# Window attention backward: the turn of P and dS of four quads moved from VectorE to a DMA transpose

## The chip, the cores and the metric

One core of a Trainium2 chip runs the program. The metric is the device time of one execution in microseconds (us); the figure for a kernel is the median of its runs. The core's engines are TensorE (PE in the profile; its weight loads are PEld), VectorE (DVE), ScalarE (ACT), GpSimd (POOL) and SyncE (SP). SP, ACT and POOL also issue DMAs. Each engine takes its instructions strictly in the order of its own queue.

## The reference

The input x is a 256 x 256 image with 384 channels in bf16, cut into 1024 windows of 8 x 8 = 64 tokens. Each window has its own one-head attention:

```
q, k, v = xw @ wqkv            # (64, 384) each
p = softmax(q @ k.T * 384**-0.5)
out = (p @ v) @ wo
```

The kernel computes `out` (out_0) and, from `grad_out`, the gradients of x (out_1), wqkv (out_2) and wo (out_3).

## The kernel before

The 1024 windows are taken in 128 *quads*. A quad is four tiles of 128 tokens, and a tile is two windows, one in partitions 0 to 63 (LO) and one in 64 to 127 (HI). The weights are multiplied together once at the start, so that the loop works with x, the output gradient d, and four 384 x 384 products A, AT, B, BT.

The order on every engine is written by hand (`manual_schedule`, L436), so each engine's queue is the program order of its instructions. The loop (L456) is a software pipeline. Step i works on three quads: A = quad i+1 is projected (y and z, L155), B = quad i gets its scores, its softmax and its u and v (L180, L192, L227), C = quad i-1 gets its attention (L254). A fourth, quad i+3, is loaded. Within a step (L346) the order is:

- scores of B on TensorE; then the softmax steps `soft` 0 to 5 on VectorE, with the exponential on ScalarE, between the four tiles of u and v, whose PSUM results ScalarE evicts (L235)
- the projection of A with kind 0 (z, evicted by ScalarE, L165), the last softmax step and `turn(B)`
- the loads of quad i+3: half of x on SP's queue (L128), the gradient on POOL's queue (L129)
- a gather of z on VectorE (L173), the projection of kind 1 (y, evicted by ScalarE, L167), the other half of the x loads on ScalarE's queue (L133)
- if there is any, one block `gf_rows` of the weight gradient on TensorE (L308), added up by VectorE (L306)
- the attention of C in four slots (L254); between the slots come half-size blocks of the weight gradient (L316), again only if there are any, and the second gather on VectorE

At the start of step i, SP's queue gets the transposing DMAs of quad i+2 (`load_turn`, L135: dT from dq and xT from xq) and of quad i (`to_tokens`, L175: tok from zy). For the first four quads dT, and for quad 0 xT, are made on TensorE instead (L143).

The softmax of a quad leaves P (called Pb) and dS, the gradient of the scores, side by side in the tile `ps` (128 x 2 x 4 x 64, bf16). Attention also needs both transposed within each window. `turn` (L237) does that on VectorE with five STREAM_TRANSPOSE instructions, which turn blocks of 32 x 32: one over the whole tile (L240) puts the diagonal blocks right, and four (L244) the off-diagonal ones. The result is the tile `PS`. One slot of attention (L263) reads it through `operand` (L247) as PT and ST, each time 64 x 64 of one half of the partitions.

All PSUM results go through one ring of eight banks (L58). In a slot of attention ScalarE evicts pw to Wq (L280), po to o (L273) and most of the d tiles; VectorE evicts pu to Uq (L283) and the d tile of the first and third slot (L273). A product can start only when an eviction has freed a bank for it.

The weight gradient is taken in groups of GQ = 3 quads. In steps 0 to 3 no group is complete, so no `gf_rows` and no half blocks are there yet. In step 127 there is no quad to project any more.

Of the kernel before, what the change touches and what calls it, by code (L numbers as in the profile page):

```python
# [9 lines left out]
ALU = mybir.AluOpType  # L10
AX = mybir.AxisListType
BF16 = mybir.dt.bfloat16
F32 = mybir.dt.float32

P = 128
WIN = 8
WT = WIN * WIN
QUAD = 4
# [5 lines left out]
def kernel(  # L24
# [21 lines left out]
    nc = tc.nc  # L46
# [8 lines left out]
    qp = ctx.enter_context(tc.tile_pool(name="qp", bufs=2))  # L55
# [64 lines left out]
    LO, HI = slice(0, WT), slice(WT, P)  # L120
# [68 lines left out]
    def over_k(ap, n=P):  # L189
        return ap.unsqueeze(2).broadcast_to([n, QUAD, WT])  # L190

    def soft(st, step):  # L192
        sd = st["sd"]
        if step == 0:
            st["mx"] = mx = sm.tile([P, QUAD], F32, tag="mx", name="mx")
            for w, h in ((0, HI), (1, LO)):
                nc.vector.tensor_reduce(out=mx[h, :], in_=sd[h, :, w, :], axis=AX.X, op=ALU.max)
        elif step == 1:
            mx = st["mx"]
            st["sh"] = sh = sm.tile([P, QUAD, WT], F32, tag="sh", name="sh")  # L200
            for w, h, o in ((0, HI, LO), (1, LO, HI)):
                nc.vector.tensor_tensor(out=sh[o, :, :], in0=sd[h, :, w, :], in1=over_k(mx[h, :], WT),
                                        op=ALU.subtract)
        elif step == 2:
            st["ex"] = ex = sm.tile([P, QUAD, WT], F32, tag="ex", name="ex")
            nc.scalar.activation(out=ex[:], in_=st["sh"][:], func=ACT.Exp)
        elif step == 3:
            ex = st["ex"]
            rs = sm.tile([P, QUAD], F32, tag="rs")
            nc.vector.tensor_reduce(out=rs[:], in_=ex[:], axis=AX.X, op=ALU.add)  # L210
            ri = sm.tile([P, QUAD], F32, tag="ri")
            nc.vector.reciprocal(out=ri[:], in_=rs[:])
            st["ps"] = ps = qp.tile([P, 2, QUAD, WT], BF16, tag="ps", name="ps")
            st["Pb"], st["dS"] = ps[:, 0, :, :], ps[:, 1, :, :]
            nc.vector.tensor_tensor(out=st["Pb"], in0=ex[:], in1=over_k(ri[:]), op=ALU.mult)
        elif step == 4:
            st["pr"] = pr = sm.tile([P, QUAD, WT], F32, tag="pr", name="pr")
            for w, h in ((0, LO), (1, HI)):
                nc.vector.tensor_tensor(out=pr[h, :, :], in0=sd[h, :, w, :], in1=st["Pb"][h, :, :], op=ALU.mult)  # L219
            st["D"] = D = sm.tile([P, QUAD], F32, tag="D", name="D")  # L220
            nc.vector.tensor_reduce(out=D[:], in_=pr[:], axis=AX.X, op=ALU.add)
        else:
            pd = sm.tile([P, QUAD, WT], F32, tag="pd")
            nc.vector.tensor_tensor(out=pd[:], in0=st["Pb"], in1=over_k(st["D"][:]), op=ALU.mult)
            nc.vector.tensor_tensor(out=st["dS"], in0=st["pr"][:], in1=pd[:], op=ALU.subtract)

    def uv(st, t, part):  # L227
# [9 lines left out]
    def turn(st):  # L237
        ps = st["ps"]
        st["PS"] = dst = qp.tile([P, 2, QUAD, WT], BF16, tag="PS", name="PS")
        nc.vector.transpose(out=dst[:].rearrange("p s t k -> p (s t k)"), in_=ps[:].rearrange("p s t k -> p (s t k)"))  # L240
        for first in range(0, P, WT):
            for q in (0, SQ):
                k = SQ - q
                nc.vector.transpose(out=dst[first + k:first + k + SQ, :, :, q:q + SQ].rearrange("p s t k -> p (s t) k"),  # L244
                                    in_=ps[first + q:first + q + SQ, :, :, k:k + SQ].rearrange("p s t k -> p (s t) k"))

    def operand(st, n, t, h):  # L247
        if n in ("PT", "ST"):
            return st["PS"][h, int(n == "ST"), t, :]
        if n in ("z", "y"):  # L250
            return st["tok"][h, int(n == "y"), :, t, :]
        return st[n][h, t, :]

    def attend(st, t):  # L254
# [8 lines left out]
        def slot(bank, straight, crossed, start=False, stop=False):  # L263
            for h in (LO, HI):
                o = OTHER[h.start]
                products = [(h, bank, straight, {"start": True, "stop": True}),
                            (o, pd[h is LO], crossed, {"start": start, "stop": stop})]
                for o, dst, (lhs, rhs), flags in products if h == LO else products[::-1]:
                    nc.tensor.matmul(dst[o, :], lhsT=operand(st, lhs, t, h), rhs=operand(st, rhs, t, h), **flags)  # L269
# [76 lines left out]
    def step(c, b, a, ahead):  # L346
# [4 lines left out]
        C_, B, A = on(c), on(b), on(a)  # L351
        B(scores)
        B(soft, 0)
        if b is not None and c is None:
            weight_rest()
        B(uv, 0, 0)
        B(uv, 0, 1)
        B(soft, 1)
        B(uv, 1, 0)
        B(uv, 1, 1)  # L360
        B(soft, 2)
        B(soft, 3)
        B(uv, 2, 0)
# [4 lines left out]
        for mo in range(CK):  # L368
            A(project, 0, mo)
        B(soft, 5)  # L370
        B(turn)
        if ahead is not None:
            load(ahead, ON_ACT)
# [16 lines left out]
    ON_ACT = 2  # L390
    EV = {"z": "AAA", "y": "AAA", "u": "AAAA", "v": "AAAA", "o": "AAAA", "U": "DDDD", "W": "AAAA", "d": "DADAA"}
    quads = [(row, col) for col in range(0, W, WIN) for row in range(0, H, 2 * WIN * QUAD)]
    sts = [{"at": q, "i": i} for i, q in enumerate(quads)]
    n = len(sts)
    AHEAD = 3
    dw_out = out_2.rearrange("(m p) j -> p m j", p=P)
    dwo_out = out_3.rearrange("(m p) n -> p m n", p=P)
# [109 lines left out]
```

## Time and profile before

| | us |
|---|---|
| median of 3 runs | 1917.22 |
| lowest and highest run | 1910.97, 1922.25 |
| the profiled execution, its own time | 1913.78 |
| its span, from the first to the last instruction | 1912.0 |
| PE, DVE, ACT, POOL busy in the span | 1897.3, 1676.1, 1530.4, 860.0 |

The span is what the profile's lines refer to; 1.8 us lie around it. Times such as "at 42.11" count from the start of the span. A line of a group of instructions names the source line, the engine, the operation, the tiles (out<-in), their shapes and types and the count; behind the bars stand the busy time in us with the mean of one instruction in ns, and the idle time of that engine before these instructions with what ended it. A line of the timeline has the start, the duration, the engine and the instruction, and in brackets how long the engine waited before it and for whom. The granted clock is TensorE's, as a share of full speed. `ACTq` and `SPq` are the queues of DMA issues. "DMA to landing" is the time from the issue of a DMA to its last byte.

### The profile page before, as it was taken

What the parts mean: (1) busy time and instruction counts of PE and PEld (TensorE: products, weight loads), DVE (VectorE), ACT (ScalarE), POOL (GpSimd) and SP (SyncE); (2) the same over time, 40 slices, a digit from 0 to 9 for tenths busy, and PEclk for the clock granted to TensorE, in tenths of its full rate; (3) what the DMA queues carried; (4) which work ended last, traced back from release to release, by engine and by line L of the source; (5) the groups of instructions that cost most, each with busy time, mean ns of one, the idle gap of its engine ahead of it and who ended that gap; (6) DMA issues with size and microseconds to landing.
All of it is one profiled execution on the core that took longest, in us unless ns stands there. A gap on an engine that the chain in (4) does not pass through costs nothing.

```text
span 1912.0 us, 57287 instructions
## 1 busy us (share of the span) xinstructions
PE 1897.3 (99%) x22359; PEld 1131.5 (59%) x22359; DVE 1676.1 (88%) x3625; ACT 1530.4 (80%) x3357; POOL 860.0 (45%) x1574
## 2 busy tenths in 40 slices
PE   8999999999999999999999999999999999999998
PEld 5556655655665565556556655655665565556555
DVE  6888888888888888888888888888888888888887
ACT  7878887888788888878887887888788788878884
POOL 3444544444444444444444444444444444445432
PEclk9999999999999999999999999999999999999999
DMA  8999999999999999999999999999999999999993
GB/s 183 200 223 215 221 211 214 232 210 222 200 232 211 225 204 229 217 223 216 224 210 212 225 226 219 206 220 221 223 214 216 223 224 204 210 231 222 206 197 93
DMA packets 943376, 406.91 MB, mean 213 GB/s; under 512 B 825344, under 2 KB 918528, under 8 KB 943104
## 3 DMA queue, kind: packets, MB, share of 16 engines
q1 hardware_dynamic: 830352, 226.46, 77.1%
q0 software_dynamic: 75264, 151.11, 32.6%
q10 hardware_dynamic: 37488, 25.67, 6.0%
q8 instruction: 175, 2.87, 0.7%
q14 instruction: 97, 0.79, 0.1%
HBM read 101.84 MB, written 101.84 MB: 107 GB/s over the span
## 4 chain that ended last, share of the span: by engine, by line
PE 95%; DVE 2%; DMA 1%; ACT 1%; issue 0%; ACTq 0%; SPq 0%
PE pj L151 50%; PE pg L151 13%; PE ph L324 13%; PE sd L151 5%; PE pw L269 5%; PE po L269 4%; PE pu L269 4%; DMA dT<-dq 1%; PE pd L269 1%; DMA xq<-in_x_dram 0%; DVE PS L244 0%; ACTq L133 0%; PE pe L403 0%; DVE pr L219 0%; DVE Uq L283 0%
## 5 line engine op out<-in xcount | busy, mean ns | idle before, releaser
L289 POOL DMA_DIRECT2D out_dram<-o x512 | 274.4, 536 | 795.4 <-ACT o L273 783.6
L280 ACT CAST Wq<-pw 128x384 bf16<-128x384 f32 x512 | 246.6, 482 | 280.7 <-PE pw L269 264.9
L151 PEld LDWEIGHTS <-xT 128*128 128x128 bf16 x3072 | 292.3, 98 | 182.9 <-issue 1.0
L129 POOL DMA_DIRECT2D dq<-in_grad_out_dram x512 | 270.6, 534 | 194.5 <-PE pj L151 86.8
L151 PE MATMUL pj<-B_sb,xT 128*128 128x384 bf16 x1536 | 334.0, 327 | 0.0
L151 PE MATMUL pj<-AT_sb,xT 128*128 128x384 bf16 x1536 | 333.8, 326 | 0.0
L283 DVE CAST Uq<-pu 128x384 bf16<-128x384 f32 x512 | 283.1, 553 | 16.9 <-PE pu L269 4.9
L291 POOL DMA_DIRECT2D out_dram<-d x480 | 277.8, 579 | 16.3 <-ACT uq L235 6.6
L151 PE MATMUL pj<-dT,BT_sb 128*128 128x512 bf16 x1152 | 269.5, 379 | 0.0
L151 PE MATMUL pj<-xT,A_sb 128*128 128x512 bf16 x1152 | 269.5, 379 | 0.0
L269 PE MATMUL pd<-tok,ps 64*64 64x384 bf16 x2048 | 256.4, 327 | 0.7 <-ACT Wq L280 0.6
L165 ACT CAST yz<-pj 128x512 bf16<-128x512 f32 x384 | 224.8, 586 | 37.2 <-PE pj L151 28.6
L273 ACT CAST o<-po 128x384 bf16<-128x384 f32 x512 | 249.3, 487 | 3.8 <-PE po L269 3.6
L235 ACT CAST vq<-pj 128x384 bf16<-128x384 f32 x512 | 247.1, 483 | 3.7 <-PE pj L151 0.5
L235 ACT CAST uq<-pj 128x384 bf16<-128x384 f32 x512 | 244.4, 477 | 3.6 <-PE pj L151 1.8
L167 ACT CAST yz<-pj 128x512 bf16<-128x512 f32 x384 | 225.1, 586 | 23.5
L244 DVE STREAM_TRANSPOSE PS<-ps 32x256 bf16<-32x256 bf16 x512 | 223.2, 436 | 9.7
L151 PEld LDWEIGHTS <-xq 128*128 128x128 bf16 x1572 | 153.6, 98 | 115.0 <-issue 0.6
L324 PEld LDWEIGHTS <-xq 64*64 64x64 bf16 x6000 | 177.5, 107 | 67.0
L324 PE MATMUL ph<-Wq,xq 64*64 64x384 bf16 x3984 | 204.4, 322 | 0.0
L151 PEld LDWEIGHTS <-A_sb 128*128 128x128 bf16 x1152 | 112.7, 98 | 135.9
L151 PEld LDWEIGHTS <-BT_sb 128*128 128x128 bf16 x1152 | 112.7, 98 | 122.3
(85 smaller groups left out, 3066.1 us busy)
## 6 DMA issues: line engine op xcount, KB each, us to landing
dq<-in_grad_out_dram POOLq DMA_DIRECT2D x512, 96.0 KB, 5.8
out_dram<-o POOLq DMA_DIRECT2D x512, 96.0 KB, 5.1
out_dram<-d POOLq DMA_DIRECT2D x480, 96.0 KB, 5.4
xq<-in_x_dram SPq DMA_DIRECT2D x262, 96.0 KB, 4.9
xq<-in_x_dram ACTq DMA_DIRECT2D x250, 96.0 KB, 6.0
out_dram<-d POOLq DMA_DIRECT2D x64, 48.0 KB, 5.4
tok<-zy SPq DMA_TRANSPOSE x128, 10.3
xT<-xq SPq DMA_TRANSPOSE x127, 7.6
```

The costliest lines, as they stand in the source:

```text
L129: nc.gpsimd.dma_start(out=dq[:, t, :], in_=windows(grad_out, st, 2 * t))
L151: nc.tensor.matmul(out, lhsT=lhsT, rhs=rhs, start=start, stop=stop)
L165: ENG[EV["z"][mo]](out=yz[:, mo, :, 0:4:3, :], in_=pj[:])
L167: ENG[EV["y"][mo]](out=yz[:, mo, :, 1:3, :], in_=pj[:])
L235: cp(out=dst[:, t, :], in_=pj[:])
L269: nc.tensor.matmul(dst[o, :], lhsT=operand(st, lhs, t, h), rhs=operand(st, rhs, t, h), **flags)
L273: copies[EV[name][i]](out=sb[rows, :], in_=src[rows, :])
L280: copies[EV["W"][t]](out=st["Wq"][:, t, :], in_=pw[:])
L283: copies[EV["U"][t]](out=st["Uq"][:, t, :], in_=pu[:])
L289: nc.gpsimd.dma_start(out=windows(out_0, st, 2 * t), in_=o)
L291: nc.gpsimd.dma_start(out=windows(out_1, st, 2 * t - 1), in_=d if t else above[:])
L324: nc.tensor.matmul(dst[o, :], lhsT=st["xq"][h, t, ma * P + o.start:ma * P + o.stop], rhs=st["UW"[f] + "q"][h, t, :], start=(i == 0), stop= ...
```

## The change

For quads 0, 1, 2 and 127 (`crossed`) the five VectorE transposes go, and one transposing DMA on SP's queue takes their place. This DMA turns 128 x 128 blocks, that is, a whole tile with both windows at once. So its source is a new tile `cr` (one buffer), in which each of the four tiles has two blocks side by side, w = 0 and w = 1: P stands in its own half of the partitions, copied there by ScalarE, and dS in the *other* half, written there by VectorE with a second subtraction of the same operands. Turned, the partitions of each half hold P of one window and dS of the same window. `operand` picks them accordingly: in the upper half PT and ST have changed places. The plain dS in `ps` is still made, since attention uses it too.

```diff
@@ soft(), last step @@
             pd = sm.tile([P, QUAD, WT], F32, tag="pd")
             nc.vector.tensor_tensor(out=pd[:], in0=st["Pb"], in1=over_k(st["D"][:]), op=ALU.mult)
+            if st["crossed"]:
+                st["cr"] = cr = qp.tile([P, QUAD, 2, WT], BF16, tag="cr", name="cr", bufs=1)
+                for w, h, o in ((0, LO, HI), (1, HI, LO)):
+                    nc.scalar.copy(out=cr[h, :, w, :], in_=st["Pb"][h, :, :])
+                    nc.vector.tensor_tensor(out=cr[o, :, w, :], in0=st["pr"][h, :, :], in1=pd[h, :, :], op=ALU.subtract)
             nc.vector.tensor_tensor(out=st["dS"], in0=st["pr"][:], in1=pd[:], op=ALU.subtract)
@@ turn() @@
         st["PS"] = dst = qp.tile([P, 2, QUAD, WT], BF16, tag="PS", name="PS")
+        if st["crossed"]:
+            whole = dst[:].rearrange("p s t k -> p (s t k)").rearrange("p (t s k) -> p t s k", t=QUAD, s=2)
+            st["PS"] = whole.rearrange("p t s k -> p s t k")
+            nc.sync.dma_start_transpose(out=whole.rearrange("p t s k -> p t (s k)"),
+                                        in_=st["cr"][:].rearrange("p t w k -> p (t w k)"))
+            return
         nc.vector.transpose(out=dst[:].rearrange("p s t k -> p (s t k)"), in_=ps[:].rearrange("p s t k -> p (s t k)"))
@@ operand() @@
-            return st["PS"][h, int(n == "ST"), t, :]
+            return st["PS"][h, int((n == "ST") == (h == LO or not st["crossed"])), t, :]
@@ the list of quads @@
-    sts = [{"at": q, "i": i} for i, q in enumerate(quads)]
-    n = len(sts)
+    n = len(quads)
+    sts = [{"at": q, "i": i, "crossed": i < GQ or i == n - 1} for i, q in enumerate(quads)]
```

## The prediction

> **What bounds the kernel now.** I read the page's first part and its 40 slices, then TensorE's waits, then 5 us windows at both ends, then the chain and the engines' timelines there.
>
> ```profile
> PE 1897.3 (99%) x22359; PEld 1131.5 (59%) x22359; DVE 1676.1 (88%) x3625; ACT 1530.4 (80%) x3357; POOL 860.0 (45%) x1574
> ```
>
> TensorE (PE) is idle for only 1912.0 - 1897.3 = 14.7 us. All of this change must come from those, from stretches at a lower clock, or from new waits. The changed quads are 0, 1, 2 and 127, so the ends matter. In the windows the columns are the window, its length, busy PE, PEld, DVE, ACT, POOL, the granted clock, DMA share and GB/s:
>
> ```profile
> 40.00:45.00 5.00, 2.96 (x39) 1.54 (x35) 4.86 (x10) 3.47 (x9) 2.60 (x5) 0.77 1.04 212
> 45.00:50.00 5.00, 5.00 (x62) 3.92 (x61) 3.22 (x9) 4.27 (x11) 4.08 (x8) 0.89 1.07 200
> ...
> 55.00:60.00 5.00, 3.29 (x53) 1.66 (x53) 4.85 (x11) 4.17 (x11) 2.33 (x4) 0.97 1.19 127
> 60.00:65.00 5.00, 5.00 (x42) 3.20 (x40) 2.07 (x5) 3.34 (x9) 4.22 (x9) 0.69 1.13 217
> ...
> 70.00:75.00 5.00, 3.29 (x62) 1.80 (x62) 4.85 (x11) 4.12 (x11) 2.42 (x5) 1.00 1.18 231
> ```
> ```profile
> 1875.00:1880.00 5.00, 3.09 (x47) 1.55 (x49) 4.77 (x10) 1.35 (x3) 0.53 (x1) 0.90 0.16 49
> 1880.00:1885.00 5.00, 5.00 (x66) 3.34 (x59) 3.16 (x6) 3.42 (x8) 3.25 (x7) 0.76 0.34 93
> ```
>
> Four holes: 2.04 us in step 1, 1.71 in step 2, 1.71 in step 3, 1.91 in step 127, each with VectorE (DVE) full. After three of them the clock falls: weighting the windows, 5 x (0.23 + 0.11) = 1.7 us, 5 x (0.03 + 0.31) = 1.7 and 5 x (0.10 + 0.24) = 1.7 are lost, 5.1 in all. Idle and clock in the steps whose turn changes are 5.7 + 5.1 = 10.8 us, the most that can be won. The chain shows what ends the first hole (start, us, what):
>
> ```profile
> 38.35 0.72 DVE PS L240
> ...
> 40.44 0.44 DVE PS L244
> 40.91 0.56 DVE zy L173
> 41.50 0.56 DVE Uq L283
> 42.09 0.57 DVE d L273
> 42.70 0.48 PE pw L269
> ```
>
> The five turns of quad 1 stand in VectorE's queue ahead of the gather and of the first eviction of attention(0), and TensorE needs that PSUM bank. Its timeline says so in step 1 and in step 127:
>
> ```profile
> 42.11 0.32 PE L269 MATMUL po<-uq,PS 64*64 64x384 bf16 x1 [1.80 <-DVE Uq L283]
> ```
> ```profile
> 1878.97 0.46 PE L269 MATMUL pu<-xq,PS 64*64 64x384 bf16 x1 [1.91 <-DVE GF_acc L306]
> ```
>
> **VectorE's part of the change.** The prices:
>
> ```profile
> L240 DVE STREAM_TRANSPOSE PS<-ps 128x512 bf16<-128x512 bf16 x128 | 91.1, 712 | 4.4
> L244 DVE STREAM_TRANSPOSE PS<-ps 32x256 bf16<-32x256 bf16 x512 | 223.2, 436 | 9.7
> L202 DVE TENSOR_TENSOR sh<-sd,mx 64x256 f32<-64x256 f32 x256 | 108.1, 422 | 8.0
> ```
>
> Removed per quad: 712 + 4 x 436 ns plus gaps, 2.56 us from 28.42 to 30.98. Added: two subtractions 64x256 into the other half of the partitions. L202 is such an operation, with the same crossing: 2 x (0.42 + 0.03) = 0.90. Net -1.66 us per quad. The L225 that stays now comes after them, which costs nothing, since dS is next read a step later.
>
> **ScalarE's part.** Two copies 64x256 in bf16, between z's and y's evictions (L165, L167). The trace has none of that shape; the nearest row is L206's 128x256 in 420 ns, after which the next eviction starts 0.32 later (24.58, then 24.90). At most 2 x 0.42 = 0.84, at least nothing where ScalarE would wait anyway; I take 0.64. In steps 1 and 2 ScalarE has hardly any slack: y's evictions are followed by two load issues and then Wq.
>
> ```profile
> 39.32 1.21 ACTq L133 DMA_DIRECT2D xq<-in_x_dram  x2
> 40.57 0.48 ACT L280 CAST Wq<-pw 128x384 bf16<-128x384 f32 x1 [0.67 <-PE pu L269]
> ```
>
> **Step 0.** There is no attention yet. Turn gone, but the second gather now waits for y's evictions, 0.64 later: they end at about 31.25 and not 30.62. mx starts at 32.5 instead of 32.70: 0.2 us won.
>
> **Step 1.** VectorE reaches Uq at 39.96 instead of 41.50 and d at 40.6 instead of 42.09. But y's third eviction ends about 0.5 later (40.4), and so do the load issues and Wq (41.1 and not 40.57). ScalarE then has eleven evictions of attention, spaced 0.37 when back to back (40.57, 40.95, 41.32), and TensorE needs their banks: the third slot's pu takes the bank of the first slot's o (free at 42.0), so it starts at 42.0 instead of 42.98. With the clock kept, ScalarE's evictions end 44.85 + 0.5, the next quad's scores start at about 45.0 instead of 46.55. Won: 1.5 us. Of the 2.04 + 1.7 in the windows the rest becomes a wait for ScalarE.
>
> **Step 2.** In the same way: Uq 1.0 earlier, Wq 0.4 later; the third pu is 57.74 instead of 58.14, scores of quad 3 59.35 instead of 59.80. They now run at full clock, ScalarE gets to uq at 61.0 instead of 62.26 and to ex at 62.5 instead of 64.61. Won: 2.0 us, more than three quarters of it clock.
>
> **Step 3** keeps its turn on VectorE and its 1.71 us; nothing is booked.
>
> **Step 127.** No projection follows, so ScalarE is idle (1.77 us before Wq at 1875.78) and hides the two copies. The gf addition moves from 1878.36 to 1876.70, pu from 1878.97 to 1877.3; po then waits until Uq ends at 1877.75. From the stop at 1877.06 to the end of that filler there remain 0.55 of idle and 2.1 of work at full clock (the step before takes 1866.03 to 1868.13 for it): 1879.7, against 1882.84. Won: 3.1 us, 1.4 idle and 1.7 clock.
>
> **The new transfer and its queue.** Four 128x128 blocks through SP's queue. The trace has twelve (xT) and twenty-four (tok):
>
> ```profile
> tok<-zy SPq DMA_TRANSPOSE x128, 10.3
> xT<-xq SPq DMA_TRANSPOSE x127, 7.6
> ```
>
> The quietest xT landed in 4.4 us, the slowest tok of the first 80 us in 14.0. Bounds for a PS transfer are therefore below 4.4 and 14.0; I take 3 to 4.4 where the engines are quiet (quads 0, 127), and "behind tok" for quads 1 and 2. Due times: PS(0) is issued at 29.5, read at 39.4; PS(1) issued at about 41, after tok(1), landing about 46, read about 53.5; PS(2) issued about 56, after tok(2), landing 63.5, read about 66.7 in the moved schedule; PS(127) issued 1876.3, read 1882.5. Nothing is late, by 1.8 us at the tightest. The first wait holds SP: load(3) issues at 30.5 instead of 23.34, and xT(3), which waited until 34.32 for ScalarE's half of the load, leaves about 0.7 later; tok and the loads behind follow by one to two microseconds with five or more in hand. If that cover went, a late tok(2) or PS(2) would give back up to 14.0 - 10.7 = 3.3 us of the gain.
>
> On the clock: the one-microsecond windows of step 1 show 0.50 from 43 to 46 us, after a wait of 1.80 us, and the sum goes by that. [...]
>
> On the transfer: the quietest xT row gives 4.4 / 12 = 0.37 us a block beside a start. [...]
>
> **Sum.** 0.2 + 1.5 + 2.0 + 3.1 = 6.8 us. The profiled execution took 1913.8 (span 1912.0 and 1.8 around it): 1907.0. The median shown is 1917.2, and the runs lie 1911 to 1922. The same kind of hole in step 3 (1.71 us) cost no clock, so the clock term depends on where the hole falls: other executions lose one to three times 1.7. From the median I book 6.8 less a third of one such stretch, about 6.2: **1911.0 us**.
>
> **Rivals.**
> 1. ScalarE becomes the bound fully, or the waits for it still halve the clock in steps 1 and 2. For: ScalarE's 4.58 of 5 busy at 65 to 70, and holes of a little over 1 us stay. Against: step 3's holes of 1.16 and 0.23 us left the clock at 1.00. Gain 0.2 + 1.0 + 0.5 + 3.1 = 4.8 less another 1.7: 3 us, 1914.
> 2. The whole 10.8 goes: ScalarE catches up because PE's banks come earlier. 1906.4 from the median.
> 3. The transfers don't help because the place of the wait merely moves (Wq instead of Uq, a hole of the same length): within 1.5 us of no change, 1916.
> 4. Slower: a PS transfer behind SP's long tok issue lands after attention wants it. It decides when PS(127) takes over 9.4 us (1885.7 - 1876.3) with quads 1 and 2 as late; at 14.0 the end loses 4.6 + 1.7 of clock, quad 2 another 3, against 0.2 + 1.5 won: +7.6, 1925. Against it: at 1875 to 1885 the DMA share is 0.16 and 0.34.
>
> **How the numbers follow.** Forecast 0.55, rival 1 0.18, rival 2 0.13, rival 3 0.08, rival 4 0.06. The range runs from rival 2 less the scatter that the runs show (1904) to rival 3 plus half of it (1919). A difference of 0.5% (9.6 us) is about what a measurement of this kernel can tell from none; the forecast lies below it. Faster by more: all of rival 2 and a tenth of the forecast and rival 1, 0.21. Slower by more: 0.04. Within: 0.75.
>
> **What would show it.** Right: TensorE's waits for Uq in steps 1 and 2 give way to shorter waits on Wq or o; the window at 1880 reads clock 1.00; the hole at step 3 is still there, some 3.5 us earlier; PS appears among the DMA issues x4 with landing below 5 us for quad 127. Wrong: a wait PE pu on DMA PS; granted clock still 0.5 at 43 to 46 or 60 to 63; load or transposes of quads 3 to 5 late; or ScalarE copies of clearly more than 0.42 us.

## The result and the profile after

The changed kernel takes **1909.48 us** (median of 16 runs, 1906.04 to 1915.17). The kernel before, in 16 runs beside them, takes 1913.57 us (1910.97 to 1922.25). The ratio is 0.9971, with a 95% interval from 0.9960 to 0.9982. So 5.5 us are won by the ratio, with 3.4 to 7.7 in the interval (the two medians lie 4.1 us apart): a real gain, below the half per cent named in the prediction. The profiled execution took 1909.96 us with a span of 1908.2, against 1913.78 and 1912.0.

The page's first part shows 7 us less work on VectorE, hardly any more on ScalarE, and 2.1 us less on TensorE. That is not less work, since the number of its instructions is the same; the clock is the likely cause, which this line alone does not show:

```profile
PE 1895.2 (99%) x22359; PEld 1128.8 (59%) x22359; DVE 1669.1 (87%) x3613; ACT 1531.9 (80%) x3365; POOL 858.4 (45%) x1574
```

The 5 us windows (columns as in the prediction) at both ends:

```profile
40.00:45.00 5.00, 4.11 (x55) 1.86 (x52) 3.73 (x8) 3.95 (x11) 1.88 (x4) 1.00 1.18 223
...
60.00:65.00 5.00, 5.00 (x30) 2.71 (x29) 3.63 (x10) 4.74 (x12) 3.38 (x7) 1.00 1.18 257
65.00:70.00 5.00, 3.48 (x38) 1.49 (x40) 4.73 (x11) 3.90 (x9) 0.52 (x1) 1.00 1.20 268
...
1875.00:1880.00 5.00, 4.46 (x88) 2.88 (x80) 4.38 (x10) 3.51 (x10) 2.93 (x6) 1.00 0.41 103
```

The granted clock (third column from the end) is 1.00 in all of them, where before it was 0.77 at 40 to 45, 0.69 at 60 to 65 and 0.90 at 1875 to 1880. TensorE's idle time in 40 to 45 falls from 2.04 to 0.89 us. At 65 to 70 the hole of step 3, whose turn is still VectorE's, stands almost as before (1.52 us idle against 1.71).

TensorE's timeline in step 1, step 3 and step 127, from three windows:

```profile
42.50 0.32 PE L280 MATMUL pd<-tok,ps 64*64 64x384 bf16 x1 [0.50 <-ACT Wq L291]
```
```profile
69.36 0.32 PE L280 MATMUL po<-uq,PS 64*64 64x384 bf16 x1 [1.28 <-DVE Uq L294]
```
```profile
1876.13 0.32 PE L280 MATMUL pd<-tok,ps 64*64 64x384 bf16 x1 [0.43 <-DVE GF_acc L317]
```

The wait of 1.80 us for Uq in step 1 has become one of 0.50 for Wq; the wait of 1.91 in step 127 is 0.43. The new operations and the transfer have these rows:

```profile
L229 DVE TENSOR_TENSOR cr<-pr,pd 64x256 bf16<-64x256 f32 x8 | 3.4, 420 | 0.2
...
L228 ACT COPY cr<-ps 64x256 bf16<-64x256 bf16 x8 | 3.2, 402 | 0.0
```
```profile
PS<-cr SPq DMA_TRANSPOSE x4, 3.0
```

The gain can be placed by the starts of the scores of each quad, the first TensorE work of a step. The columns: start of quad 1's scores, then the length of the stretches between starts, the tail from quad 127's scores to the end, and the span. Every kernel below is in it but the one with all quads crossed, whose middle is not the same code; the table is read from TensorE's timeline.

| us | quad 1 at | 1 to 2 | 2 to 3 | 3 to 4 | 4 to 5 | 7 to 127 | tail | span |
|---|---|---|---|---|---|---|---|---|
| before | 30.51 | 16.04 | 13.25 | 14.82 | 14.57 | 1749.99 | 43.29 | 1912.0 |
| before, second trace | 29.69 | 16.02 | 13.30 | 14.77 | 14.56 | 1754.99 | 42.07 | 1914.5 |
| after | 30.81 | 15.14 | 12.44 | 13.37 | 15.44 | 1751.23 | 40.59 | 1908.2 |
| after, second trace | 29.83 | 15.10 | 12.44 | 13.37 | 14.57 | 1748.81 | 40.62 | 1903.9 |
| last quad alone | 30.07 | 16.01 | 13.42 | 14.64 | 14.57 | 1750.20 | 40.28 | 1908.3 |
| first three alone | 30.14 | 15.02 | 12.44 | 13.37 | 14.57 | 1750.27 | 41.87 | 1906.8 |
| loads first | 30.11 | 14.51 | 12.45 | 13.50 | 14.57 | 1751.52 | 40.56 | 1906.3 |
| copies on VectorE | 30.70 | 15.53 | 13.18 | 14.35 | 15.16 | 1750.09 | 40.96 | 1909.1 |
| first four | 29.70 | 14.81 | 12.47 | 12.46 | 16.99 | 1752.88 | 40.54 | 1909.0 |
| four, loads first | 29.68 | 14.78 | 12.45 | 12.83 | 19.43 | 1751.06 | 40.52 | 1909.9 |
| four, quad 7's loads on SP | 30.73 | 15.04 | 12.48 | 13.27 | 15.82 | 1749.81 | 40.52 | 1907.0 |
| the same, loads first | 30.65 | 14.39 | 12.44 | 13.26 | 15.89 | 1750.15 | 40.55 | 1906.5 |

An undisturbed step takes 14.57 us. The stretch from quad 7 to quad 127, the same code in all of these kernels, varies by 6 us between executions, and quad 1 starts up to 1 us apart. So one trace's span says nothing below a few microseconds, while the short stretches of the same code repeat to 0.2 us wherever the clock does. From quad 1 to quad 4 before takes 44.11 and 44.09, after 40.95 and 40.91: **3.2 us won at the start**. The tail takes 43.29 and 42.07 before, 40.59 and 40.62 after: **2.7 or 1.5 won at the end**.

How much of the gain is clock can be estimated from all runs, since each lists its mean granted clock. A stretch at half clock lasts 3.41 us in the traces and lowers the mean by 0.0009. In the 77 runs of the kernel before that stand beside the experiments the mean is 0.9978, in the changed kernel's 16 runs 0.9994. The difference is 3.2 us of lost work at most, of the 4.1 to 5.5 won. Those 77 runs reach from 0.994 to 1.000, so the clock is not halved the same number of times in each execution.

### The profile page after: what moved, and what is told of

Read it like the earlier page. It is cut to its first block, busy times and chain, and to the rows that moved or that the text cites. A ratio compares the mean times of both kernels' runs of the same rounds, so it can differ in the third digit from the quotient of the medians.

```text
span 1908.2 us, 57297 instructions
## 1 busy us (share of the span) xinstructions
PE 1895.2 (99%) x22359; PEld 1128.8 (59%) x22359; DVE 1669.1 (87%) x3613; ACT 1531.9 (80%) x3365; POOL 858.4 (45%) x1574
## 4 chain that ended last, share of the span: by engine, by line
PE 95%; DMA 2%; ACT 1%; DVE 1%; ACTq 0%; issue 0%; SPq 0%
PE pj L151 50%; PE pg L151 13%; PE ph L335 13%; PE sd L151 5%; PE pw L280 5%; PE po L280 4%; PE pu L280 4%; DMA dT<-dq 2%; PE pd L280 1%; ACTq L133 0%; DMA xq<-in_x_dram 0%; PE pc L105 0%; PE pe L414 0%; ACT yz L167 0%; ACT Wq L291 0%
## 5 line engine op out<-in xcount | busy, mean ns | idle before, releaser
L255 DVE STREAM_TRANSPOSE PS<-ps 32x256 bf16<-32x256 bf16 x496 | 216.2, 436 | 9.4
```

## The experiments

The theory on trial: what is won is VectorE's queue in front of the first evictions of attention, in steps 1, 2 and 127 separately, partly as idle time and partly as clock; in steps 1 and 2 ScalarE's loads and evictions take over as the next limit. The rivals: the gain belongs to one end alone; the copies on ScalarE or the place of the loads hold back more than the turn did; the transfer itself is what is late.

**1. The last quad alone.**

```diff
-"crossed": i < GQ or i == n - 1
+"crossed": i == n - 1
```

> Only quad 127 is crossed; quads 0 to 2 keep VectorE's turns. If the two ends are won separately, the scores of quad 127 start where they start before (1868.7 in that trace) and the 2.9 us between them and the attention of quad 127 go as they do in the changed kernel: about 2.9 us below before, a ratio of 0.9985. If the end counts only because the start had moved the granted clock's phase, the second half-clock stretch at the end is back and 1.4 us or less are won, a ratio of 0.9993 or more.

Measured: 1911.40 us, ratio to before 0.9987 [0.9973, 1.0002]. The tail is 40.28, as short as in the changed kernel, with the clock at 1.00; the start is 44.07, as before, with the clock down (0.70 at 40 to 45, 0.75 at 60 to 65). So the end is won without the start. In the times the gain of the end alone is too small for its interval.

**2. The first three alone.**

```diff
-"crossed": i < GQ or i == n - 1
+"crossed": i < GQ
```

> Only quads 0, 1 and 2 are crossed. The start should win as in the changed kernel: the scores of quad 4 about 2.9 us earlier than in the trace of before. Theory 1 (SP's queue slipped and the middle of the run takes most of it back): 1 to 1.5 us remain at the scores of quad 127 and at the end, a ratio of 0.9993. Theory 2 (what the middle took was scatter of that one execution): about 2.9 us remain, 0.9985. The hole of 1.91 us and the low clock at the end are there as before.

Measured: 1911.13 us, 0.9995 [0.9975, 1.0014]. The start is 40.83, as in the changed kernel. The hole of step 127 is back, of exactly the old length, but it does not cost clock this time. The timeline of TensorE and the windows there:

```profile
1875.19 0.32 PE L280 MATMUL pu<-xq,PS 64*64 64x384 bf16 x1 [1.91 <-DVE GF_acc L317]
```
```profile
1870.00:1875.00 5.00, 3.28 (x43) 1.73 (x41) 4.74 (x11) 1.58 (x4) 0.53 (x1) 1.00 0.53 125
1875.00:1880.00 5.00, 4.69 (x74) 3.08 (x74) 4.22 (x9) 3.33 (x8) 3.26 (x7) 1.00 0.30 87
```

Before, the same 1.91 us were followed by 0.76. The tail is 41.87 and not 43.29. The clock term of the end is therefore not a property of the hole's length. Which of the two theories on the whole holds, 1 to 1.5 us or 2.9, the times can't tell: the interval holds either, and no gain as well.

**3. The loads ahead of the turn.** The loads of quad i+3 go ahead of the transposing DMA in SP's queue.

```diff
-        B(turn)
         if ahead is not None:
             load(ahead, ON_ACT)
+        B(turn)
```

> The changed kernel, with the loads of quad i+3 put ahead of the turn, so that the new DMA no longer stands before them in SP's queue; the other engines' order stays. Theory 1: the x loads of quads 3, 4 and 5 issue at about 24, 41 and 55 instead of 31.0, 43.6 and 59.1, ScalarE no longer waits before the Wq of step 4 (2.7 us in the changed kernel), the lead at the scores of quad 5 stays within 0.3 us of that at quad 4, and the time is 1 to 1.7 us below the changed kernel, a ratio of about 0.9965 to before. Theory 2: no difference to the changed kernel, 0.997.

Measured: 1910.23 us, 0.9977 [0.9962, 0.9993]. Step 1 is 14.51 instead of 15.14. ScalarE's queue there, first of the changed kernel, then of this one:

```profile
40.58 1.35 ACTq L133 DMA_DIRECT2D xq<-in_x_dram  x1
41.97 0.48 ACT L291 CAST Wq<-pw 128x384 bf16<-128x384 f32 x1 [1.05 <-PE po L280]
```
```profile
39.88 0.73 ACTq L133 DMA_DIRECT2D xq<-in_x_dram  x1
40.65 0.48 ACT L291 CAST Wq<-pw 128x384 bf16<-128x384 f32 x1 [0.43 <-PE pu L280]
```

The issue of ScalarE's second x load takes 1.35 us in the one and 0.73 in the other. In the changed kernel PS(0) stands ahead of load(3) in SP's queue, so xT(3) leaves at 36.09 (34.32 before), and the long issue of tok(1) lies at 37.62 to 42.23, over ScalarE's load. With the loads first, tok(1) is issued from 35.98 to 40.26 and ends in the middle of that load. That this overlap lengthens the issue is argued and not shown: in step 2 of the changed kernel tok(2) is issued from 51.72 to 57.68, and ScalarE's load within it takes 0.62. The 0.6 us are there in the trace, and too few for the times, whose intervals overlap; the expected 1.0 to 1.7 us below the changed kernel are not seen.

**4. The changed kernel, unchanged, once more.**

> The changed kernel once more, for a second trace. Theory 1: between the scores of quads 4 and 5 again 0.5 to 1 us of the lead is lost behind a late Wq of step 4, and one to two us more before quad 127. Theory 2: the losses stand at other steps or are missing.

Measured: 1905.67 us, span 1903.9. Start and tail repeat to 0.04 us. Step 4 takes 14.57 and not 15.44: the loss of 0.87 us in the first trace is not in each execution. So the second theory fits. Experiments 6 to 10 show what the loss is.

**5. The copies on VectorE.**

```diff
-nc.scalar.copy(out=cr[h, :, w, :], in_=st["Pb"][h, :, :])
+nc.vector.tensor_copy(out=cr[h, :, w, :], in_=st["Pb"][h, :, :])
```

> The changed kernel with the two copies of P on VectorE instead of ScalarE; everything else as changed. In the changed kernel VectorE idles 0.64 us before Uq in steps 1 and 2, so two short bf16 copies (0.1 to 0.42 us each by the rows of the gather and of L206) hide there. Theory A (ScalarE's queue sets the end of attention in steps 1 and 2): z and y are evicted without a gap, the x loads and Wq come 0.6 us earlier, and from the scores of quad 1 to those of quad 4 the trace needs 40.1 to 40.5 us, against 40.9 in the changed kernel and 44.1 before. Theory B (VectorE still sets it): 40.9 or more. At the end ScalarE was idle, so there the copies cost VectorE 0.3 to 0.8 us.

Measured: 1911.77 us, 0.9979 [0.9963, 0.9995]. A copy takes 218 ns on VectorE, against 402 on ScalarE, and yet the start is longer, 43.06 instead of 40.95. The number is that of theory B, but VectorE is not what sets it in step 1: the longest wait of TensorE there, 0.52 us at 42.05, is for ScalarE's Wq. ScalarE is relieved of 0.82 us and comes to its loads earlier, during SP's issue of tok(1) (36.95 to 41.55), but the two issues take 1.97 us, against 1.21 before, and Wq starts at 41.52. The clock then falls (0.72 at 45 to 50, 0.67 at 70 to 75). So the expected gain did not come. Why the two issues are long here the runs do not show.

**6. The first four and the last.**

```diff
-"crossed": i < GQ or i == n - 1
+"crossed": i < 4 or i == n - 1
```

> Quads 0 to 3 and 127 are crossed. The changed kernel's step 3 still has holes of 1.28, 0.24 and 0.25 us behind VectorE's turn of quad 3. If the change works by taking the turn out of VectorE's queue, these shrink to less than 0.8 in all and the scores of quad 4 come 0.6 to 1.0 us earlier than in the changed kernel: 40.0 to 40.3 us after the scores of quad 1, against 40.9. If ScalarE's queue takes over, 40.7 or more.

Measured: 1909.08 us, 0.9979 [0.9963, 0.9996]. The hole of step 3 goes, as expected: quad 1 to quad 4 takes 39.74, 1.2 less than after. But step 4 takes 16.99, 2.4 more than an undisturbed one. ScalarE's queue shows where:

```profile
78.14 4.77 ACTq L133 DMA_DIRECT2D xq<-in_x_dram  x2
82.95 0.48 ACT L291 CAST Wq<-pw 128x384 bf16<-128x384 f32 x1 [4.24 <-DMA xq<-in_x_dram]
```

The two load issues of quad 7 last 4.77 us, and the evictions of attention stand behind them. The first starts at 78.14, the second only at 82.37, and the trace names as its releaser the transposing DMA dT(6), which left SP at 75.07, behind PS(3), took 7.3 us and landed at 82.35. The data can't be the reason: the load does not touch dT, and `xq` has ten buffers, of which quad 7's had not been used. What ties the load to dT(6) the traces do not show. The same wait is the loss of the changed kernel's first trace, where the first of the two issues has it. There dT(6) left at 73.46 and took 8.4, and the load was issued at 81.84:

```profile
81.84 1.84 ACTq L133 DMA_DIRECT2D xq<-in_x_dram  x2
83.73 0.48 ACT L291 CAST Wq<-pw 128x384 bf16<-128x384 f32 x1 [2.68 <-PE po L280]
```

Before, dT(6) landed at 81.7 and ScalarE came to the load only at 83.3, so that 1.6 us were in hand. Who wins three microseconds ahead of step 4 has used these up, unless dT(6) lands earlier too: in the second trace of the changed kernel it landed at 78.88 and nothing was lost.

**7. All quads crossed.**

```diff
-"crossed": i < GQ or i == n - 1
+"crossed": True
```

> All 128 quads are crossed, so the copies, the 1.2 us of SP's queue and the four extra blocks beside 48 come in every step, and VectorE's 1.66 us go in every step. Theory A (the middle is bound by TensorE, and all of this hides): the steps stay at 14.57 us, the time within 3 us of the changed kernel, 0.997 to before. Theory B (the transposing DMAs and ScalarE's queue have too little room in a step): steps of 14.8 us or more, 1.01 or above, with TensorE waiting for Wq or for tok.

Measured: 1938.37 us in 4 runs (1919.86 to 1945.28), ratio 1.0134 [1.0103, 1.0164]: 1.3% slower. The profiled run is the fastest of them and shows only part of the loss: 16.54 us for step 4 and 19.76 for step 6, while quad 7 to quad 127, 1756.1, is hardly above the scatter of the table. VectorE and ScalarE wait for `cr`, which has one buffer, until the PS transfer before has read it (in all, times, longest):

```profile
DVE cr L229 <- DMA PS<-cr: 29.4, 13, 5.4
...
ACT cr L228 <- DMA PS<-cr: 21.0, 10, 4.7
```

Beside the regular transfers a PS transfer takes 5.0 us in the median and not 3.0. TensorE's matmuls wait for PS for only 0.6 us in all, and VectorE is relieved by some 60 us per 500 without any gain: in the steady part VectorE's turns lie beside other work and can't be won. That the queue for the transposes and the one buffer of `cr` make the loss is argued from these rows; no kernel with a second buffer was run, and the three slower runs have no trace.

**8. The first four, loads ahead of the turn** (the edits of 3 and 6 together).

> Quads 0 to 3 and 127 crossed, and the loads ahead of the turn in SP's queue, the two edits that the traces point to. From the scores of quad 1 to those of quad 4: 39.4 to 39.9 us (40.9 less 0.4 for the loads and 0.6 to 1.0 for the turn of quad 3). The whole: 1.0 to 1.5 us below the changed kernel, about 0.9963 to before, unless scatter in the middle hides it.

Measured: 1912.51 us, 0.9988 [0.9969, 1.0007]. The start is 40.06 and missed its expectation. Step 4 takes 19.43, 4.9 too long: ScalarE's load of quad 7 is issued at 82.11, when dT(6) has landed (73.58 and 8.5 us), although its last eviction of y had ended at 79.02. After the hole that follows, the clock is halved from 84.92 to 88.33, which is up to 1.7 of the 4.9 us. dT(6) landed at nearly the same time as in kernel 6 (82.09 against 82.35), but there only the second load stood behind it and here both do: their issues follow it with 1.92 us, and Wq starts at 84.07 against 82.95.

**9 and 10. Quad 7's x loads on SP.** The kernels of 6 and of 8, and in step 4 all four x loads go to SP's queue:

```diff
-            load(ahead, ON_ACT)
+            load(ahead, 0 if ahead["i"] == 7 else ON_ACT)
...
-            load_rest(ahead, ON_ACT)
+            load_rest(ahead, 0 if ahead["i"] == 7 else ON_ACT)
```

> Quads 0 to 3 and 127 crossed, and the two x loads of quad 7 that ScalarE issues in step 4 go to SP's queue; all else as in the kernel with the first four crossed. Theory A (in step 4 ScalarE stands with its first x load of quad 7 behind the landing of dT(6), and its evictions of attention behind that): the wait is gone from ScalarE's queue, step 4 takes 14.6 to 15.0 us instead of 16.99, and from the scores of quad 1 to those of quad 5 it is 54.4 to 54.9 us (56.7 with the first four, 56.4 after, 58.7 before); Wq of step 4 at most 0.5 us after its product. Rival B (what is late in step 4 is the data: dT(6) or xT for the projection, or a bank): the load's place makes no difference, step 4 stays at 16.5 to 17.5 with TensorE waiting for a DMA. Time by A: 1.5 to 2 us below the changed kernel, 1907 to 1908, ratio to before 0.996 to 0.997; by B 1909 to 1910.

> Quads 0 to 3 and 127 crossed, the x and gradient loads issued ahead of the turn, and quad 7's x loads all on SP's queue. Theory A (ScalarE's load behind dT(6) is the whole of the 4.9 us that step 4 lost in the kernel without the last edit): step 4 takes 14.6 to 15.0 instead of 19.43, scores of quad 1 to quad 5 54.6 to 55.1 instead of 59.5. Rival B (late data): 18 us or more stay. Time by A: like the kernel with the first four and quad 7's loads on SP, 1907 to 1908; by B 1911 to 1913.

Measured: 1908.83 us, 0.9973 [0.9953, 0.9992], and 1907.62 us, 0.9969 [0.9949, 0.9989]. The wait is gone from ScalarE's queue, in both. In kernel 9 (start, duration, what, and in brackets the wait before it):

```profile
83.72 0.48 ACT L291 CAST Wq<-pw 128x384 bf16<-128x384 f32 x1 [1.67 <-PE pw L280]
```

ScalarE now waits for TensorE's product, as in every ordinary step. So it was the load's place and not late data. But step 4 is still 15.82 and 15.89 and not the 14.6 to 15.0 expected, and quad 1 to quad 5 takes 56.61 and 55.98 where 54.4 to 55.1 was expected; kernel 6 took 56.73. The reason is another one, the clock. TensorE in one-microsecond windows of kernel 9 (length, busy, granted clock, DMA share, GB/s):

```profile
70.00:71.00 1.00, 0.94 (x13) 0.89 1.26 305
71.00:72.00 1.00, 1.00 (x18) 0.50 1.30 218
...
73.00:74.00 1.00, 1.00 (x4) 0.50 1.14 343
74.00:75.00 1.00, 1.00 (x7) 0.90 1.12 374
```

The granted clock is 0.50 from 70.79 to 74.20, over the end of step 3 and the beginning of step 4. Of that, 71.52 to 74.20 lies in step 4 and costs about 1.3 us; without it the step would take 14.5. Kernel 10 has the same from 70.15 to 73.57. Their ratios to before, 0.9973 and 0.9969, can't be told from the changed kernel's 0.9971: no version that was tried is shown to beat it.

**11. The kernel before, once more.**

> The kernel before, unchanged, for a second trace. If the halved clock after the holes of steps 1, 2 and 127 depends on where the holes fall, some of the four holes cost clock here and others not, and the steps that are not halved are about 1.5 us shorter: scores of quad 1 to quad 4 between 41 and 44.2 us, the tail from the scores of quad 127 between 41.8 and 43.3. If it depends on the length of a hole alone, the same three stretches show it again (44.1 and 43.3). Quads 7 to 127: 1749 to 1753, as in the other traces.

Measured: 1916.34 us, span 1914.5. The start is 44.09 with the clock down in both places, as in the first trace. At the end the hole is there in its old length, at 1882.71, and the clock stays:

```profile
1882.71 0.32 PE L269 MATMUL pu<-xq,PS 64*64 64x384 bf16 x1 [1.91 <-DVE GF_acc L306]
```
```profile
1880.00:1885.00 5.00, 2.97 (x60) 1.80 (x56) 4.37 (x10) 2.13 (x7) 1.52 (x3) 1.00 0.07 20
```

The tail is 42.07. So the end is worth 2.7 us when the clock halves after the old hole, and 1.5 when it does not: of three traces with that hole, it halved in one.

## Why the prediction was right

The forecast was 1911.0 with a gain of 6.2 us; measured were 1909.48, and 5.5 us by the ratio (4.1 between the medians). The mechanism is the one predicted, at all the places named but step 0; one wait that was not on its list, ScalarE's load in step 4, came on top. Some sizes were off, and two errors stood against each other, so that the forecast came within 1.5 us of the measurement is in part luck.

- **The base.** The forecast started from the median of three runs, 1917.22. Sixteen runs have 1913.57, which is 3.65 lower. That made the forecast too high; the gain, booked 2.1 above the difference of the medians, made it too low by less. 1911.0 - 3.65 + 2.1 is 1909.5.
- **Steps 0 and 1**, booked with 0.2 and 1.5: together 0.90 in the stretch from quad 1 to quad 2. From quad 0's scores to quad 1's nothing changes (12.20 in both). Quad 1's mx (the maxima of its scores) does start earlier, 1.75 us after its first score against 2.19, but z's evictions on ScalarE start 0.19 later, so this does not reach TensorE. Step 1 is the term that was mis-sized. Wq starts 11.16 us after quad 1's scores, against 10.06 before: 1.1 later and not the 0.5 forecast. Of this 0.72 stand at y's third eviction, behind copies that cost 0.82 and not the 0.64 booked; the rest is the second x load on ScalarE, which alone took 1.35 us where a two-load issue took 1.21 before. Experiment 3 gives 0.63 back by moving SP's queue alone.
- **Step 2 with the clock of step 3**, booked with 2.0, more than three quarters of it clock: 0.81 from quad 2 to 3, and 1.45 from quad 3 to 4, together 2.26. The waits there are now 0.15 us.
- **Step 3 keeps its hole**: right, 1.28 us at 69.36 and two short ones behind it. With the fourth quad crossed it goes (13.37 to 12.46).
- **Step 127**, booked with 3.1 (1.4 idle and 1.7 clock): 2.70 over the tail of the first traces, with 0.43 of idle left where 0.55 was forecast. The idle part is 1.45 against the second trace of before, as booked; the clock part came in one of three traces. By these three, two thirds of a stretch would have been due off the sum at the end alone; the forecast took off one third in all.
- **The transfer**: PS lands in 2.5 and 3.0 us for quads 0 and 127, at or below the lower end of "3 to 4.4", and in 3.1 and 6.0 for quads 1 and 2; no product waits for it in the changed kernel. Rival 4 is refuted at four quads. With all 128 crossed there is a loss; that it comes by way of `cr` and the queue is argued.
- **"tok and the loads behind follow by one to two microseconds with five or more in hand"**: the slip was larger, load(4) left 3.4 us later than before and load(5) 5.2 later. No data was late. What the list of due times lacked is an issue that waits: ScalarE's own load in step 4 stands behind the landing of dT(6), with 1.6 us in hand and not five. It cost 0.87 in one trace and nothing in the other.
- **Rival 1** (ScalarE bound) is half true: ScalarE ends the waits of step 1 now, but the clock stayed at 1.00. **Rival 2** (all 10.8) fails: the stretches of the first traces add up to 5.9, and 0.89 us are still idle at 40 to 45. **Rival 3** fails: the holes did not move, they shrank.

On the transfer: the four blocks of PS land in 3.0 us together in the median of four transfers (2.5 to 6.0), and the quietest xT of the first 80 us of before, twelve blocks, in 4.4 (4.1 over its whole trace).

On the clock: the halved stretches last 3.41 us (42.65 to 46.06, 59.72 to 63.13 and 1879.02 to 1882.43 before, 70.79 to 74.20 in kernel 9), with a granted clock of 0.50. In the 3.41 us ahead of the three before, TensorE was busy for 1.43, 1.78 and 1.50 us; in kernel 9 it was busy for 2.77, and the profile lists only two waits there (0.16 and 0.24 us, and 0.15 and 0.30 in kernel 10). The busy time alone does not tell them from others: before, it was busy for 1.98 us from 69.96 to 73.37, over the hole of step 3, and for 1.64 us in the 3.41 us from 1871.64 with the first three alone, over the hole of step 127, and both times the clock stayed at 1.00. Nor does the length of the wait: after the 1.91 us of step 127 the clock halved in one of three traces. The two stretches of the start were there in both traces of before and with the last quad alone. So the clock terms that the prediction read from one trace came again at the start, and not each time at the end. That they depend on where a hole falls was its author's reading; what decides it no run here shows.

Open is the scatter from quad 7 to quad 127, 1748.8 to 1755.0 in the same code, which is larger than the whole gain in a single pair of traces.

## What to carry to other kernels

Relieving a busy engine pays where its work stands ahead of something that the bound engine needs next (the first steps and the last one here), and not where it lies beside other work: four quads won 5.5 us, all 128 lost 1.3%. When work moves to a DMA queue, write out for each later step what every engine's next DMA issue waits for, and how much is in hand; the 1.6 us in hand of step 4 were worth as much as a hole. Take what a hole costs in clock from several traces: after the same hole of 1.91 us the clock halved in one of three. Judge small edits by the stretches that they touch, aligned at their start, and a median by many runs, not by the span of one trace.

## What had not been expected of the hardware

- An issue on ScalarE's queue of an x load takes 0.59 us in the median (0.61 before), but over 0.8 us in 52 of the changed kernel's 250 and in 50 of before's 250, and up to 1.47 and 2.41 us. Nearly all of the issues, long and short, 246 and 245, overlap one of SP's of the 24 blocks of tok, so this overlap alone does not tell the long from the short; what does is open.
- A 64x256 copy in bf16 takes 218 ns on VectorE and 402 on ScalarE.
- The granted clock fell to 0.50 for 3.41 us after holes of steps 1, 2 and 127 in the first trace of before, and stayed at 1.00 after the hole of step 3 there and after the same 1.91 us of step 127 in two other traces. In kernel 9 it fell after 2.77 us busy in 3.41. Neither the length of the wait nor TensorE's busy time in the 3.41 us ahead (1.43 to 2.77 before the halvings, 1.64 and 1.98 where the clock stayed) tells the one from the other; what does is open.
